# A kernel of attention and MLP on one Trainium2 core: another dealing of weight pieces, another order of MLP blocks, idle products, and an earlier order of v

## The chip, the cores and the metric

The kernel runs on 1 core of one Trainium2 chip. The metric is the device time of one execution in microseconds (us). A time is given as the median of the runs with the lowest and highest in brackets. All runs quoted here are of the fast state, but for one of `budget_mid_xt_first`, which is named there.

Before: 677.28 us (677.25 to 677.75, 3 runs).

## The reference, cut to what matters

```python
# attention, q k v f_logit: (4 batches, 8 heads, 768 tokens, 48)
f = 1 / (1 + exp(-f_logit))
for t in range(S):
    state = f[:, :, t, :, None] * state + einsum('bhd,bhe->bhde', k[:, :, t], v[:, :, t])
    y[:, :, t] = einsum('bhd,bhde->bhe', q[:, :, t], state)
x = y.transpose(0, 2, 1, 3).reshape(3072, 384)
# MLP, w_in: 384 x 2048, w_out: 2048 x 384 (scaled by numpy to float64)
h = x @ w_in
out = (h * sigmoid(1.702 * h)) @ w_out
```

## The kernel before

The sequence is cut into 12 attention units of 256 tokens. Each unit loads f, q and k (`raw`) and v (`vn`, and one `vl` per level), makes scores level by level, then the states (`st`), then the result `y`. ScalarE copies y out of PSUM into `yT`, and six DMA orders bring it into `xT`, the MLP's input. The MLP products (`h = xT @ w_in`, `o = g @ w_out`) of earlier units are put between the attention parts as filling, counted in columns. A whole MLP of a unit is `UNIT` = 24576 columns, some 41 us of TensorE by the 0.43 us that 256 columns took.

The weights arrive as float64 bits and are turned to float32 on VectorE: 32 pieces, in pairs of ten steps. Pieces are converted beside the first four attention units, and MLP blocks (a quarter of a unit's MLP each) can only be run when their pieces are done.

```python
def load_raw(n, j, engine=nc.sync):          # f, q or k of unit n: four orders on one queue
    ...
def load_vn(n): ...                          # v of unit n: from the third unit on, one order
def to_x(y, x, ng):                          # yT to xT: six orders on the same queue
    for h in range(2):
        most, rest = y(h)
        nc.sync.dma_start(out=x[h * D:(h + 1) * D]..., in_=most)          # L591
        ... nc.sync.dma_start(out=x[D2 + p:D2 + p + w, c]..., in_=...)    # L596, twice

def mlp_h(n, ffs, g):
    ...
    return [(U, lambda ff=ff, c=c: one(ff, c), ...) for ff in ffs for c in range(NK)]

# in the attention unit n (cut): the order in which its loads are sent
#   "states":     if n + 1 >= N_TURN: load_vn(n + 1)
#   begin_k:      if n: load_raw(n + 1, 2)       # k, run at the end of unit n - 1
#   "inter":      y += state products; yT copies; to_x(...)

def merge(n, fill, columns, share, pieces=0, hold=0, by=1.0):
    ...   # the parts of unit n, with `columns` of filling and `pieces` conversions between them
    converting = {"W": 3, "T": 3, "B": 1} if n < N_FILL - 1 else {"W": 3, "V": 4, "S": 3, "T": 1, "B": 1}
    ...

merge(0, fill, 0, steady, 8)
fill += mlp_blocks((0, 0)) + mlp_blocks((0, 1))
merge(1, fill, UNIT // 2 - LAG // 2, steady, 10, hold=1)
fill += mlp_blocks((1, 0), (1, 1)) + mlp_blocks((0, 2), (1, 2))
merge(2, fill, UNIT, steady, 8)
fill += mlp_blocks((2, 0), (2, 1)) + mlp_blocks((2, 2), (0, 3)) + mlp_blocks((1, 3), (2, 3))
merge(3, fill, 3 * UNIT // 2 - LAG // 2, steady, 6, by=0.7)
```

The units are called first to twelfth below; the first is n = 0. "States end" is the end of the last L542 of a unit. Other lines that come up: L383 the scores (`sc`), L562 the products of y with the states, L570 the copies of y into `yT`, L619 the products h, L645 the products o, L625 on VectorE the gate (`g`, from h and its sigmoid), L218 to L227 the weight conversions. In a kernel with an edit ahead of a line its number is up to seven higher (L626 for L619, say).

Of the kernel before, what the change touches and what calls it, by code (L numbers as in the profile page):

```python
# [9 lines left out]
F32 = mybir.dt.float32  # L10
# [13 lines left out]
def kernel(  # L24
# [32 lines left out]
    nc = tc.nc  # L57
    B, H, S, D = q.shape
    DM = H * D
    DFF = moe_w_in.shape[1]  # L60
    P = 128
    C = 64
    G = 128
    U = 256
# [6 lines left out]
    NL = len(LEV)  # L71
    NK = DM // P
    NFF = DFF // P
    FG = 4
    PAIRS_AHEAD = 3
    N_FILL = 3
# [10 lines left out]
    ps = ctx.enter_context(tc.tile_pool(name="ps", bufs=1, space=bass.MemoryType.PSUM))  # L87
# [16 lines left out]
    ident = const.tile([P, P], F32, name="ident")  # L104
# [3 lines left out]
    masks = const.tile([P, NL, 64], F32, name="masks")  # L108
# [40 lines left out]
    for r in range(NGR):  # L149
        ffs = range(r * FG, (r + 1) * FG)  # L150
        for ff in ffs[::2]:
            f = slice(ff * P, (ff + 2) * P)
# [8 lines left out]
    NPC = 2 * FG  # L161
# [68 lines left out]
    def convert():  # L230

        if state["begin"] < len(pairs) and len(todo) <= NOP:
            begin_pair(state["begin"])
            state["begin"] += 1
        if todo and todo[0]:
            todo.pop(0)()
        if todo and todo[0] is None:
            todo.pop(0)
            state["done"] += 2
            fetch_weights()  # L240
# [34 lines left out]
    def load_vl(n, l):  # L275

        if n >= NALL:
            return
        t = vls[n, l] = ld.tile([P, DM], F32, tag=f"vl{l}", name=f"vl_{n}_{l}")
        if n < N_TURN:  # L280
            pt = ps.tile([P, DM], F32, tag="mm", name=f"tv_{n}_{l}", bufs=4)
            for g in range(NG):
                nc.tensor.matmul(  # L283
                    pt[g * 64:(g + 1) * 64], lhsT=perm[:, l - 1, :] if l else ident[:, ::2], rhs=vns[n][:, g, :],
                    start=True, stop=True,
                )
            nc.scalar.copy(t, pt)
            return
        nc.sync.dma_start(out=t, in_=v_toks[n % 2].rearrange("(n two m) e -> two n m e", two=2, m=LEV[l])[0])
# [20 lines left out]
    serial = count()  # L310
# [295 lines left out]
    def width(n):  # L606

        return U + (n == NALL - 1)

    def mlp_h(n, ffs, g):  # L610
        t = {}

        def one(ff, c):
            if c == 0:
                if ff % FG == 0:
                    g[ff // FG] = mlp.tile([P, FG, width(n)], F32, tag="g", name=f"g_{n}_{ff}", bufs=6)
                t["ph"] = ps.tile([P, width(n)], F32, tag="mm", name=f"h_{n}_{ff}", bufs=4)
            ph = t["ph"]
            nc.tensor.matmul(  # L619
                ph, lhsT=w_in[:, c, ff * P:(ff + 1) * P], rhs=xTs[n][:, c, :], start=(c == 0), stop=(c == NK - 1)  # L620
            )
            if c == NK - 1:
                sg = mlp.tile([P, width(n)], F32, tag="sg", name=f"sg_{n}_{ff}")
                nc.scalar.activation(sg, ph, AF.Sigmoid, scale=1.702)  # L624
                nc.vector.tensor_tensor(g[ff // FG][:, ff % FG, :], ph, sg, ALU.mult)  # L625
                if width(n) > U:  # L626

                    by = g[ff // FG][:, ff % FG, U:]
                    if ff == 0:
                        g["last"] = mlp.tile([P, 1, DM], F32, tag="sum", name="sum_last", bufs=3)  # L630
                        nc.vector.tensor_scalar(g["last"][:, 0], w_out[:, 0, :], by, None, op0=ALU.mult)
                    else:
                        nc.vector.scalar_tensor_tensor(
                            g["last"][:, 0], w_out[:, ff, :], by, g["last"][:, 0], op0=ALU.mult, op1=ALU.add
                        )
        return [(U, lambda ff=ff, c=c: one(ff, c), ff // FG * NPC + ff % FG + 1) for ff in ffs for c in range(NK)]

    def mlp_o(n, ffs, g, done):

# [39 lines left out]
    def mlp_block(n, r):  # L679

        g, ffs = {}, range(r * FG, (r + 1) * FG)

        def done(tt, po):
            if r == 0 and tt == 0:
                sums[n] = mlp.tile([P, U // P, DM], F32, tag="sum", name=f"sum_{n}", bufs=3)
            acc = sums[n][:, tt]
            if r == 0:
                nc.scalar.copy(acc, po)
            else:
                nc.vector.tensor_tensor(acc, acc, po, ALU.add)  # L690
            if r == NGR - 1:
                store(n, tt, acc)
        return mlp_h(n, ffs, g), mlp_o(n, ffs, g, done)

    def mlp_blocks(*blocks):

        hs, os = zip(*(mlp_block(n, r) for n, r in blocks))
        return sum(hs, []) + sum(os, [])


    units = [attention(n) for n in range(NALL)]
    LAG = 18 * DM

    def parts_of(n):

        parts = list(units[n][1])
        _, inter = parts.pop()
        if n:
            kind, scores = parts[0]
            _, ahead = units[n - 1][1][-1]  # L710
            parts[0] = kind, lambda: (ahead(), scores())
        if n < N_TURN:

            def with_v(l):
                kind, fn = parts[l]
                return kind, lambda: (fn(), load_vl(n, l) if n == 0 or l else None)
            parts[:NL] = [with_v(l) for l in range(NL)]
        if n + 1 < NALL:
            begin_f, begin, begin_k, begin_gates = units[n + 1][0]
            i = len(parts)  # L720
            if n + 1 < N_FILL:

                parts.append(("K", lambda: (begin_k(), begin_gates(), load_vl(n + 1, 0) if n + 1 < N_TURN else None)))
                parts.insert(i - 4, ("B", begin))
                parts.insert(i - 5, ("B", begin_f))
            else:
                kind, states = parts.pop()
                parts += [("B", begin_k), (kind, lambda: (states(), begin_gates()))]
                parts.insert(i - 3, ("B", lambda: (begin_f(), begin())))
        else:  # L730
            parts.append(("W", inter))
        return parts

    def merge(n, fill, columns, share, pieces=0, hold=0, by=1.0):



        parts = parts_of(n)
        total = sum(share(kind) for kind, _ in parts)
        converting = {"W": 3, "T": 3, "B": 1} if n < N_FILL - 1 else {"W": 3, "V": 4, "S": 3, "T": 1, "B": 1}  # L740
        total_ops = sum(converting.get(kind, 0) for kind, _ in parts)
        held = sum(share(kind) for kind, _ in parts[:hold])
        at = at_ops = done = ops = 0
        for kind, fn in parts:
            ready = state["done"]
            fn()
            at += share(kind)
            at_ops += converting.get(kind, 0)
            n_ops = min(int(pieces * NOP * at_ops / (by * total_ops)), pieces * NOP) - ops
            ops += n_ops  # L750
            first, n_columns = done, max(0, columns * (at - held) / (total - held) - done)

            def some(end):
                nonlocal done
                while fill and done < end and fill[0][2] <= ready:
                    w, emit, _ = fill.pop(0)
                    emit()
                    done += w
            for i in range(n_ops):
                some(first + n_columns * i / n_ops)  # L760
                convert()
            some(first + n_columns)
# [4 lines left out]
    UNIT = NFF * NK * U + U // P * NFF * DM  # L767
# [12 lines left out]
        load_raw(1, j)  # L780
    load_vn(1)
    fill = []
    merge(0, fill, 0, steady, 8)
    fill += mlp_blocks((0, 0)) + mlp_blocks((0, 1))
    merge(1, fill, UNIT // 2 - LAG // 2, steady, 10, hold=1)
    fill += mlp_blocks((1, 0), (1, 1)) + mlp_blocks((0, 2), (1, 2))
    merge(2, fill, UNIT, steady, 8)
    fill += mlp_blocks((2, 0), (2, 1)) + mlp_blocks((2, 2), (0, 3)) + mlp_blocks((1, 3), (2, 3))
    merge(3, fill, 3 * UNIT // 2 - LAG // 2, steady, 6, by=0.7)
    fill_order.close()  # L790
    for n in range(3, NALL):
        fill += mlp_unit(n)
# [33 lines left out]
```

## Time and profile before

| | before |
|---|---|
| time | 677.28 us (677.25 to 677.75) |
| span of the profile | 674.0 us |
| TensorE busy | 652.6 us |
| states end, first, second, third unit | 43.9, 84.8, 141.4 us |
| TensorE at half clock, 11 to 160 us | 13.7 us |

The last row is from the table by stretch in steps of half a microsecond. The share of the chain of work that ended last, by engine:

```profile
PE 89%; DVE 7%; ACT 2%; issue 1%; DMA 1%; SPq 0%; DVEq 0%; ACTq 0%
```

DMA has 1% of it. The DMA queue's own view, in order of time, round the end of the second unit (start, length of the order on the queue, line, what is moved, how many):

```profile
72.52 0.69 SPq L289 DMA_DIRECT2D vl<-v_tok  x1
74.29 5.47 SPq L179 DMA_DIRECT2D bits<-in_moe_w_out_dram  x2
79.85 0.57 SPq L289 DMA_DIRECT2D vl<-v_tok  x1
80.47 0.46 SPq L303 DMA_DIRECT2D vn<-v_tok  x1
83.12 2.58 SPq L257 DMA_DIRECT2D raw<-in_k_dram  x4
87.07 0.59 SPq L591 DMA_DIRECT2D xT<-yT  x1
87.70 1.22 SPq L596 DMA_DIRECT2D xT<-yT  x2
89.12 0.51 SPq L591 DMA_DIRECT2D xT<-yT  x1
90.57 1.38 SPq L596 DMA_DIRECT2D xT<-yT  x2
```

I did not read this view before predicting; it is shown here because the case turned on it. The reader is to see the order: v of the third unit, the four orders of k of the fourth unit, then the six of xT. The yT copies began at 85.28, and the last xT landed at 93.88 by the chain: 8.6 us later. A length here is only the time of the order on the queue, not that to the landing: below, an order of 0.46 us lands after 13.66.

### The profile page before, as it was taken

To read this page: it belongs to the slowest core of one execution; us is meant where nothing else is said; L and a number is where in the kernel's file an instruction comes from. 1 tells how busy PE (TensorE), PEld (TensorE's weight loads), DVE (VectorE), ACT (ScalarE), POOL (GpSimd) and SP (SyncE) were. 2 spreads that over 40 slices of the span, in tenths; PEclk is the share of its full clock that TensorE was granted. 3 is DMA by queue.
4 is the path that set the end of the run, shared out by engine and by line. 5 is a ranking of instruction groups with operands and counts; after the bars stand their busy time and mean duration, and the time that the engine had idled before them with its cause. 6 is when DMAs were issued, how large, how long until landed. Compare 5 with 4: busy or idle time off the path is not lost.

```text
span 674.0 us, 19354 instructions
## 1 busy us (share of the span) xinstructions
PE 652.6 (97%) x8514; PEld 486.5 (72%) x8514; DVE 378.4 (56%) x675; ACT 226.4 (34%) x459; POOL 50.3 (7%) x116
## 2 busy tenths in 40 slices
PE   5879999999999999999999999999999999999997
PEld 4656766757777886886886886876886786786774
DVE  3999877887666546545546546445446444430440
ACT  4564443343134233333333233233233233231210
POOL 3020020010002002002002002002002001000000
PEclk9789999999999999999999999999999999999999
DMA  8877973571063535415415415415414103001000
GB/s 193 226 192 193 240 160 89 152 185 37 24 159 107 154 66 149 109 38 148 115 33 152 110 37 148 113 37 144 115 37 115 37 24 84 15 1 36 13 1 24
DMA packets 67551, 67.62 MB, mean 100 GB/s; under 512 B 30410, under 2 KB 61290, under 8 KB 67466
## 3 DMA queue, kind: packets, MB, share of 16 engines
q1 hardware_dynamic: 67466, 66.38, 38.6%
q8 instruction: 67, 1.10, 0.7%
q14 instruction: 18, 0.15, 0.1%
HBM read 56.92 MB, written 8.65 MB: 97 GB/s over the span
## 4 chain that ended last, share of the span: by engine, by line
PE 89%; DVE 7%; ACT 2%; issue 1%; DMA 1%; SPq 0%; DVEq 0%; ACTq 0%
PE h L619 37%; PE o L645 35%; PE sc L383 5%; PE y L447 5%; PE t L338 2%; PE y L562 2%; PE tkn L504 1%; PE sc L522 1%; DVE s L218 1%; DVE A L409 1%; DMA xT<-yT 1%; PE tv L283 1%; ACT yT L570 1%; DVE X L436 1%; DVE X L438 1%
## 5 line engine op out<-in xcount | busy, mean ns | idle before, releaser
L619 PE MATMUL h<-xT,w_in 128*128 128x256 f32 (+1 forms) x1152 | 261.1, 382 | 1.1 <-DVE sum L690 0.8
L645 PE MATMUL o<-w_out,g 128*128 128x384 f32 x768 | 259.6, 491 | 0.9 <-DVE g L625 0.9
L619 PEld LDWEIGHTS h<-xT,w_in 128*128 128x128 f32 x1152 | 215.8, 190 | 36.8 <-issue 3.5
L645 PEld LDWEIGHTS o<-w_out,g 128*128 128x128 f32 x768 | 143.0, 190 | 94.5 <-issue 2.2
L625 DVE TENSOR_TENSOR g<-h,sg 128x256 f32<-128x256 f32 (+1 forms) x192 | 80.8, 422 | 133.1 <-ACT sg L624 132.6
L624 ACT ACTIVATE sg<-h 128x256 f32<-128x256 f32 (+1 forms) x192 | 73.2, 383 | 169.4 <-PE h L619 164.1
L422 ACT COPY Kc<-X 128x512 f32<-128x512 f32 x69 | 45.9, 666 | 123.7 <-DVE X L438 87.3
L438 DVE TENSOR_TENSOR X<-X,tot 128x1024 f32<-128x1024 f32 x45 | 55.2, 1226 | 54.8 <-PE sc L383 50.1
L409 DVE TENSOR_TENSOR A<-sc,masks 128x512 f32<-128x512 f32 x72 | 46.7, 679 | 0.0
L326 DVE STREAM_TRANSPOSE X<-raw 128x1024 f32<-128x1024 f32 x18 | 36.7, 2039 | 16.7 <-PE y L562 13.9
L447 PE MATMUL y<-A,vl 64*48 64x64 f32 x2304 | 41.7, 219 | 0.0
L447 PEld LDWEIGHTS y<-A,vl 64*48 64x48 f32 x2304 | 36.8, 122 | 5.3 <-issue 5.0
L375 POOL TENSOR_TENSOR tot<-F 128x512 f32<-128x512 f32 x12 | 12.5, 1039 | 340.5 <-DVE st L539 327.9
L383 PE MATMUL sc<-X,Kc 48*64 48x64 f32 x1344 | 29.0, 224 | 6.8 <-ACT Kc L422 4.6
L383 PEld LDWEIGHTS sc<-X,Kc 48*64 48x64 f32 x1344 | 24.6, 138 | 13.8 <-ACT Kc L422 7.2
L570 ACT COPY yT<-y 48x512 f32<-48x512 f32 x48 | 27.8, 580 | 20.0 <-PE y L562 19.4
L331 ACT ACTIVATE F<-F 128x1024 f32<-128x1024 f32 x9 | 9.5, 1057 | 49.0 <-DVE F L326 49.0
L375 POOL TENSOR_TENSOR tot<-tot 128x256 f32<-128x256 f32 (+4 forms) x60 | 23.7, 395 | 4.7
L542 DVE TENSOR_TENSOR st<-st,sc 128x192 f32<-128x192 f32 x44 | 15.6, 354 | 15.1 <-PE sc L522 13.7
L338 PE MATMUL t<-ident,raw 128*64 128x128 f32 x288 | 19.6, 298 | 4.4 <-DMA raw<-in_f_logit_dram 4.4
L338 PEld LDWEIGHTS t<-ident,raw 128*64 128x64 f32 x288 | 18.4, 153 | 7.0 <-issue 6.1
L664 ACT COPY osb<-o 128x384 f32<-128x384 f32 x18 | 8.6, 478 | 41.5 <-PE o L645 41.5
(66 smaller groups left out, 385.0 us busy)
## 6 DMA issues: line engine op xcount, KB each, us to landing
vl<-v_tok SPq DMA_DIRECT2D x60, 192.0 KB, 2.8
bits<-in_moe_w_out_dram SPq DMA_DIRECT2D x8, 768.0 KB, 9.8
bits<-in_moe_w_in_dram SPq DMA_DIRECT2D x8, 576.0 KB, 7.9
v_tok<-in_v_dram SPq DMA_DIRECT2D x10, 384.0 KB, 4.3
vn<-v_tok SPq DMA_DIRECT2D x10, 384.0 KB, 6.0
xT<-yT SPq DMA_DIRECT2D x24, 144.0 KB, 2.7
raw<-in_f_logit_dram SPq DMA_DIRECT2D x18, 192.0 KB, 3.9
raw<-in_q_dram SPq DMA_DIRECT2D x18, 192.0 KB, 3.1
```

Source lines behind the costliest of these rows:

```text
L326: nc.vector.transpose(out.rearrange("p (a i j) -> p a j i", a=NP, j=R), raw[:, j].rearrange("p a (j d) -> p (a j) d", j=R)[:, :, :32],)
L338: nc.tensor.matmul(pt[h * HS:(h + 1) * HS, jj, :], lhsT=by_pair[j][:, h, x:x + HS], rhs=ident, start=True, stop=True)
L375: nc.gpsimd.tensor_tensor(tn, t2[:, :, 0], t2[:, :, 1], ALU.mult)
L383: nc.tensor.matmul(out[g * HS:(g + 1) * HS, h, a, :], lhsT=lhs(h, a * U + g * G), rhs=rhs(h, a * U + g * G), start=True, stop=True,)
L409: nc.vector.tensor_tensor(A[:, :, c:c + w].rearrange("p h (x t) -> p h x t", t=64), t["sc"][:, :, c:c + w].rearrange("p h (x t) -> p h x t ...
L422: nc.scalar.copy(c.rearrange("p (n m) -> p n m", m=m), X[:, j, :NA].rearrange("p (n two m) -> p n two m", two=2, m=m)[:, :, hf, :],)
L438: nc.vector.tensor_tensor(qk, qk, by, ALU.mult)
L447: nc.tensor.matmul(dst(h, g, a), lhsT=vls[n, u][g * 64:(g + 1) * 64, (2 * a + h) * D:(2 * a + h + 1) * D], rhs=A(h, g, a), start=(start an ...
L619: nc.tensor.matmul(ph, lhsT=w_in[:, c, ff * P:(ff + 1) * P], rhs=xTs[n][:, c, :], start=(c == 0), stop=(c == NK - 1))
L624: nc.scalar.activation(sg, ph, AF.Sigmoid, scale=1.702)
L625: nc.vector.tensor_tensor(g[ff // FG][:, ff % FG, :], ph, sg, ALU.mult)
L645: nc.tensor.matmul(t["po"], lhsT=g[ff // FG][:, ff % FG, tt * P:(tt + 1) * P], rhs=w_out[:, ff, :], start=(ff == ffs[0]), stop=(ff == ffs[ ...
```

## The change

The intent is to spread the weight conversions more evenly over the first four units (6, 6, 12, 8 pieces for 8, 10, 8, 6), so that the first unit, in which VectorE is the bound (busy for all of the 17 us from 17 to 34), and the second get shorter. The filling of these units shrinks with it, and the MLP blocks come in the order in which their weights are ready. Small parts go along: orders of v earlier, five idle products that are to keep the array's clock up, and the three products of an h as one piece of filling.

```diff
-        return [(U, lambda ff=ff, c=c: one(ff, c), ...) for ff in ffs for c in range(NK)]
+        return [(NK * U, lambda ff=ff: [one(ff, c) for c in range(NK)], ...) for ff in ffs]
...
+    def keep_up(times):
+        pt = ps.tile([P, NL * 64], F32, tag="mm", name=f"idle_{next(serial)}", bufs=4)
+        for _ in range(times):
+            nc.tensor.matmul(pt, lhsT=ident, rhs=masks.rearrange("p l t -> p (l t)"), start=True, stop=True)
...
-                return kind, lambda: (fn(), load_vl(n, l) if n == 0 or l else None)
+                ls = (l,) if n == 0 else {0: (1, 2, 3), 1: (4,), 2: (5,)}.get(l, ())
+                return kind, lambda: (fn(), [load_vl(n, i) for i in ls], keep_up(2 - l // 2) if n == 0 and l < 3 else None)
...
-        converting = {"W": 3, "T": 3, "B": 1} if n < N_FILL - 1 else ...
+        converting = {"W": 3, "T": 2, "B": 1, "K": 2} if n < N_FILL - 1 else ...
...
-    merge(0, fill, 0, steady, 8)
-    fill += mlp_blocks((0, 0)) + mlp_blocks((0, 1))
-    merge(1, fill, UNIT // 2 - LAG // 2, steady, 10, hold=1)
-    fill += mlp_blocks((1, 0), (1, 1)) + mlp_blocks((0, 2), (1, 2))
-    merge(2, fill, UNIT, steady, 8)
+    merge(0, fill, 0, steady, 6)
+    fill += mlp_blocks((0, 0))
+    merge(1, fill, UNIT // 8, steady, 6, hold=1)
+    fill += mlp_blocks((1, 0)) + mlp_blocks((0, 1), (1, 1)) + mlp_blocks((0, 2), (1, 2))
+    merge(2, fill, UNIT * 7 // 8, steady, 12)
     fill += mlp_blocks((2, 0), (2, 1)) + mlp_blocks((2, 2), (0, 3)) + mlp_blocks((1, 3), (2, 3))
-    merge(3, fill, 3 * UNIT // 2 - LAG // 2, steady, 6, by=0.7)
+    merge(3, fill, 2 * UNIT - LAG // 2, steady, 8, by=0.5)
```

Below, "the plan" is the dealing, the budgets of columns, the order of blocks and the table `converting`.

More of the change, by code (lines that the diff above doesn't have):

```diff
@@ L635, in one @@
                         )
-        return [(U, lambda ff=ff, c=c: one(ff, c), ff // FG * NPC + ff % FG + 1) for ff in ffs for c in range(NK)]
+        return [(NK * U, lambda ff=ff: [one(ff, c) for c in range(NK)], ff // FG * NPC + ff % FG + 1) for ff in ffs]
     def mlp_o(n, ffs, g, done):
@@ L739, in merge @@
         total = sum(share(kind) for kind, _ in parts)
-        converting = {"W": 3, "T": 3, "B": 1} if n < N_FILL - 1 else {"W": 3, "V": 4, "S": 3, "T": 1, "B": 1}
+        converting = {"W": 3, "T": 2, "B": 1, "K": 2} if n < N_FILL - 1 else {"W": 3, "V": 4, "S": 3, "T": 1, "B": 1}
         total_ops = sum(converting.get(kind, 0) for kind, _ in parts)
```

## The prediction

> **What bounds the kernel now.** I read the page's busy shares first, then the table by stretch, then the order of time of VectorE and TensorE where the table shows a gap. The page:
>
> ```profile
> PE 652.6 (97%) x8514; PEld 486.5 (72%) x8514; DVE 378.4 (56%) x675; ACT 226.4 (34%) x459; POOL 50.3 (7%) x116
> ```
>
> TensorE is busy for 652.6 of 674.0 us, so only 21.4 us is idle. From 209 us on it never waits, apart from the last 3.5 us (the final store). Hence nothing after the first quarter can gain: no product of the real work is removed. The table by stretch (stretch, length, busy us of PE, PEld, DVE, ACT, POOL, then granted clock, DMA share, GB/s):
>
> ```profile
> 12.46:20.00 7.54, 4.35 (x104) 2.19 (x104) 7.06 (x15) 2.87 (x7) 2.06 (x5) 1.00 1.08 261
> 23.00:28.50 5.50, 5.00 (x85) 3.83 (x85) 5.50 (x14) 2.64 (x6) 0.00 (x0) 0.50 0.75 177
> 28.50:38.60 10.10, 9.33 (x292) 7.56 (x290) 10.10 (x24) 7.12 (x13) 0.38 (x2) 1.00 0.92 234
> 44.80:47.50 2.70, 0.03 (x3) 0.01 (x2) 2.55 (x5) 2.63 (x6) 2.39 (x5) 0.64 0.32 70
> 47.50:52.40 4.90, 4.90 (x72) 3.27 (x73) 4.53 (x11) 2.05 (x4) 0.10 (x1) 0.50 0.53 114
> 52.40:84.00 31.60, 31.60 (x532) 22.55 (x530) 27.73 (x65) 15.45 (x32) 0.38 (x2) 1.00 0.88 221
> ```
>
> Two things are to be seen. In the first attention unit (12.5 to 44 us) VectorE is busy without a break: it bounds there, TensorE only looks busy. And twice TensorE runs at half clock, 21.7 to 28.5 and 45.6 to 52.4 us. What VectorE does in the first unit, in order of time (start, length):
>
> ```profile
> 29.69 0.68 DVE L435 TENSOR_TENSOR X<-X,tot 128x512 f32<-128x512 f32 x1
> 30.35 0.69 DVE L436 TENSOR_TENSOR X<-X,tot 128x512 f32<-128x512 f32 x1
> 30.95 0.68 DVE L409 TENSOR_TENSOR A<-sc,masks 128x512 f32<-128x512 f32 x1
> 31.55 0.62 DVE L225 TENSOR_SCALAR a<-s 128x384 int32<-128x384 int32 x2
> 32.09 1.02 DVE L226 SCALAR_TENSOR_TENSOR a<-bits,a 128x384 f32<-128x384 uint32 x2
> 33.03 1.02 DVE L227 TENSOR_TENSOR w_out<-a,s 128x384 f32<-128x384 f32 x2
> ```
>
> A level costs 1.8 us of its own work (L435, L436, L409 follow at 0.60), and then the weight conversions (L218 to L227). From starts: a pair of L222 or L225 takes 0.54, a pair of L218, L226 or L227 0.94. Ten such steps, one pair of pieces, take 3.90 us. And TensorE around its gaps:
>
> ```profile
> 20.64 0.69 PE L383 MATMUL sc<-X,Kc 48*64 48x64 f32 x32 [1.96 <-ACT Kc L422]
> 47.49 1.13 PE L383 MATMUL sc<-X,Kc 48*64 48x64 f32 x32 [2.67 <-ACT Kc L422]
> 151.72 4.69 PE L619 MATMUL h<-xT,w_in 128*128 128x256 f32 x20 [0.78 <-DVE sum L690]
> ```
>
> [...]
>
> **The change part by part.** I walked the new order of VectorE and TensorE with the durations above.
>
> *First unit, 6 pieces for 8.* Ahead of the states (L537) VectorE now has 31 conversion steps for 44. The 13 removed are one pair (3.90) plus one L222 (0.27) and two L218 (0.94): 5.1 us, all on the path. The first levels stay as they were, because the copy Kc waits behind two activations for a weight DMA that lands at 18.98. By the walk the states end at 39.1 for 43.9.
>
> *Idle products.* Five of 128x384. A product of that shape takes 0.645 us (32 records, 16 products, in 10.32 us), 3.2 us together. Two fall into the gap of 1.64 us at 15.1, two into that of 1.96, one into 0.5. They hide behind VectorE and should keep the clock up; but 3.15 us of cold time saved there is gain only where TensorE bounds, so I count none.
>
> *Orders of v early.* Three products of v (0.8 us each) move into the 2.67 us gap where ScalarE copies yT (4 x 0.58) and Kc. The gap shrinks to some 0.4, and the second cold stretch (4.9 us busy at half clock, so 2.45) should go.
>
> *Second unit.* Steps 50 to 30, and the fill falls from 8832 columns to 3072; 256 columns of a product take 0.43 us, and so TensorE has 24 us of work for 34. VectorE has 30 x 0.39 = 11.7, 18 x 0.6 = 10.9, gates 1.4 and 0.6 lost to GpSimd's turn: 24.6 us. It now bounds, and waits some 2.5 us for the first gate: the first h needs xT, which landed 6.5 us after the yT copies began. States end 39.1 + 27.2 + 3.1 (eight L539/L542) = 69.4 (before: 84.8, with 10.4 us more MLP done).
>
> *Third unit.* Steps 35 to 55. VectorE: 55 x 0.39 = 21.5, 18 x 0.6 = 10.8, twelve gates 4.1, sums 1.0, three transposes 5.8, a promotion 1.15 and 0.6: 45 us, against 40 for TensorE. It bounds again; with 2.8 us of waits the states end at 69.4 + 47.8 + 3.1 = 120.3. Before it was 141.3, having done 8 h (1.3 each) and 8 o (0.65) more: 15.6 us. Like for like 125.7 becomes 120.3: **5.4 us gained**, nearly all from the first unit.
>
> *Fourth unit.* Here I expect a new wait. After the first scores come eight h in a row, and the four PSUM buffers "mm" let only four (5.2 us) run before the first gate has freed one. That gate stands on VectorE behind ten conversion and sum steps (4.3), two promotions with the ScalarE copies between (3.8), two evacuations (1.2) and GpSimd's turn (some 1.3): 10.8 us after the states. TensorE is there after 6.5: a wait of 4.3 us, where before 16 o came first and 0.78 was lost. **Cost 3.5 us**, and the clock may fall in it (3 chances in 4, some 2.5 us: 1.9). *Products of an h together* only shifts points of interleaving by under 0.9 us; I count zero.
>
> Sum: -5.4 + 3.5 + 1.9 = 0.0, so by the bare walk 677.3.
>
> **The rivals.** (1) *TensorE takes the whole saving*: the conversions hide in the third and fourth units, and most idle time between 12 and 152 us (some 13.5 us) plus the cold 5.6 goes. For it: VectorE is only 56% busy over the span. Against: those units would be at 45 of 48 us. It would give 660 to 664. (2) *VectorE becomes the bound of unit three*, with transposes and sums behind conversions holding PSUM buffers: idle time only moves. For it the sums above. 675 to 680. (3) *Weight DMA paces it*: the DMA share is near 1 up to 45 us, and conversions wait. Against: pieces are needed later than before, and only 2.5 us of waiting for bits is in the trace. No change, 677.
>
> **Range and chances.** The walk charges each wait in full and lets nothing slip by, and eighths of a unit look like numbers tuned by measurement; so between the walk (677.3) and half of rival 1's gain I choose a gain of 3.3 us: 674.0. One wait of 4 us more or less on each side and an uncertain clock give 667 to 679. For 2% the gain would have to be 13.5 us, nearly all there is: 0.04. A loss of 13.5 us would need several new waits like that of the fourth unit: 0.01.
>
> **What would show it.** Right: the first states end near 39 us; the clock is full to 45 us; the gap ahead of the second unit's second scores is under 1 us; VectorE is 90% busy or more from 70 to 118 us; and an h in the fourth unit waits 3 to 5 us for a gate L625, perhaps with half clock after it. From then on no waits. Wrong: if that wait is under 1 us the time is near 669; if TensorE is idle under 2 us in the third unit, VectorE's steps overlap better than I walked; if cold stretches stay in the first two units, idle products do not do what they are for, and the time is above 677.

## The result, and the profile after

The changed kernel took **687.02 us** (683.47 to 688.08, 4 runs) beside 677.51 us (677.25 to 679.1, 4 runs) of the kernel before. The ratio is 1.0126, 95% interval 1.0084 to 1.0168. A ratio is the mean time of one kernel's fast runs over the mean of the other's of the same rounds, so it is not quite the ratio of the medians. In a later job the same kernel took 684.5 us (`after_again` below). It is slower by about 1%, within the 2% of "same", and outside the predicted range.

The page of the changed kernel, busy shares and then the chain that ended last:

```profile
PE 659.2 (96%) x8524; PEld 491.5 (72%) x8524; DVE 381.5 (56%) x675; ACT 227.1 (33%) x459; POOL 51.3 (7%) x116
...
PE 82%; DVE 7%; DMA 6%; SPq 2%; ACT 1%; issue 1%; DVEq 0%; ACTq 0%
```

The span grew by 12.1 us in this execution: TensorE is busy 6.6 us longer (4.7 of it the idle products) and idle 5.5 us longer. DMA with its queue has gone from 1% of the chain to 8%. What TensorE waited for:

```profile
PE h L619 <- DMA xT<-yT: 5.1, 2, 2.6
...
PE y L562 <- issue: 3.4, 2, 1.7
PE y L562 <- DVE st L542: 3.0, 2, 2.5
PE h L619 <- DVE g L625: 1.7, 1, 1.7
```

Two waits for xT, 5.1 us together, are new: before, that row had 0.3. The DMA queue in order of time, at the same place as before:

```profile
70.34 0.82 SPq L179 DMA_DIRECT2D bits<-in_moe_w_in_dram  x2
71.26 0.56 SPq L289 DMA_DIRECT2D vl<-v_tok  x1
71.88 0.46 SPq L303 DMA_DIRECT2D vn<-v_tok  x1
73.04 3.51 SPq L257 DMA_DIRECT2D raw<-in_k_dram  x4
79.08 0.59 SPq L591 DMA_DIRECT2D xT<-yT  x1
80.29 4.63 SPq L596 DMA_DIRECT2D xT<-yT  x2
85.60 0.52 SPq L591 DMA_DIRECT2D xT<-yT  x1
86.16 1.83 SPq L596 DMA_DIRECT2D xT<-yT  x2
```

The yT copies began at 77.04, so the first order should go near 79 and the last near 82. Instead the queue stands still between 80 and 85.6. The chain says on what:

```profile
71.88 13.66 DMA vn<-v_tok
...
85.60 2.94 DMA xT<-yT
...
88.68 5.81 PE h L619 x18
```

The load of v took 13.66 us to land, and the fourth order of xT is sent at the moment it has landed. Why the one should wait for the other is told by counting orders. The queue's waits of this trace name, for the xT orders, weights (2.5 us), a vl (3.5) and vn (0.6). Going back eight orders from the first xT one comes to a weight load, from the third to the vl of 71.26, from the fourth to vn. By this count an order of xT that stood still went out when the order eight before it had landed. The packed trace, which also holds what `prof` does not print, says why: the program has eight semaphores for the landing of its orders and deals them out in turn, so that in both kernels each of the 347 later orders (of 355) signals the same one as the order eight before it, and the xT orders that stood still waited for just that one. In both traces all 347 went out after the last landing signal of the order eight before; in the changed kernel the third of xT at 84.42 us, the vl having landed at 84.40, and the fourth at 85.60, vn having landed at 85.54. That comes from this program's eight semaphores; no run here shows a limit of the chip. In the kernel before the same count holds: there two xT orders waited, for 1.2 us together, for loads of k, which are eight back from the fifth and sixth.

The changed kernel stretches its loads over less time. From the vl order ahead of q's four to the end of k's orders it takes 14.2 us (62.37 to 76.55), and before the same run of orders, with one weight order more, took 19.9 us (65.78 to 85.70). The stretch of 18 us round it, before and then after, by the table by stretch (length, busy us of PE, PEld, DVE, ACT, POOL, clock, DMA share, GB/s):

```profile
72.00:90.00 18.00, 17.11 (x305) 12.62 (x294) 15.67 (x37) 10.49 (x21) 3.63 (x6) 1.00 0.94 223
```

```profile
72.00:90.00 18.00, 12.92 (x201) 8.88 (x196) 12.35 (x26) 7.04 (x12) 3.19 (x6) 0.89 0.80 156
```

TensorE lost 4 us in these 18, and VectorE 3. The clock fell too, from 1.00 to 0.89.

Where the span went, from the ends of the states. The walk is the one of the prediction; its last part is that of before with the 15.6 us of moved MLP work, 3.5 for the fourth unit's wait and 1.9 for the clock added, so that its sum is, as in the prediction, the span of before:

| | before | the walk | after |
|---|---|---|---|
| first unit's states end | 43.9 | 39.1 | 40.4 |
| second unit | 40.9 | 30.3 | 34.5 |
| third unit | 56.6 | 50.9 | 59.4 |
| from there to the end | 532.6 | 553.6 | 551.8 |
| span | 674.0 | 673.9 | 686.1 |

### The profile page after: what moved, and what is told of

It is laid out like the page before. It is cut to its first block, busy times and chain, and to the rows that moved or that the text cites. A ratio compares the mean times of both kernels' runs of the same rounds, so it can differ in the third digit from the quotient of the medians.

```text
span 686.1 us, 19380 instructions
## 1 busy us (share of the span) xinstructions
PE 659.2 (96%) x8524; PEld 491.5 (72%) x8524; DVE 381.5 (56%) x675; ACT 227.1 (33%) x459; POOL 51.3 (7%) x116
## 4 chain that ended last, share of the span: by engine, by line
PE 82%; DVE 7%; DMA 6%; SPq 2%; ACT 1%; issue 1%; DVEq 0%; ACTq 0%
PE h L619 35%; PE o L645 34%; PE sc L383 4%; PE y L447 4%; DMA vn<-v_tok 2%; PE y L562 2%; PE sc L522 1%; DMA bits<-in_moe_w_out_dram 1%; PE tkn L504 1%; DMA bits<-in_moe_w_in_dram 1%; DMA xT<-yT 1%; DVE s L218 1%; DVE a L226 1%; SPq L179 1%; SPq L250 1%
## 5 line engine op out<-in xcount | busy, mean ns | idle before, releaser
L619 PEld LDWEIGHTS h<-xT,w_in 128*128 128x128 f32 x1152 | 218.9, 192 | 44.0 <-issue 6.4
L625 DVE TENSOR_TENSOR g<-h,sg 128x256 f32<-128x256 f32 (+1 forms) x192 | 81.1, 424 | 152.4 <-ACT sg L624 151.7
L505 ACT COPY kn<-tkn 128x512 f32<-128x512 f32 x24 | 13.8, 583 | 36.0 <-PE tkn L504 35.9
L356 POOL COPY q_last<-X 128x4 f32<-128x4 f32 x12 | 10.3, 859 | 188.1 <-DVE X L326 139.1
L542 DVE TENSOR_TENSOR st<-st,sc 128x192 f32<-128x192 f32 x44 | 15.6, 354 | 14.7 <-PE sc L522 13.2
## 6 DMA issues: line engine op xcount, KB each, us to landing
vn<-v_tok SPq DMA_DIRECT2D x10, 384.0 KB, 13.7
```

Source lines behind the costliest of these rows:

```text
L619: nc.tensor.matmul(ph, lhsT=w_in[:, c, ff * P:(ff + 1) * P], rhs=xTs[n][:, c, :], start=(c == 0), stop=(c == NK - 1))
L625: nc.vector.tensor_tensor(g[ff // FG][:, ff % FG, :], ph, sg, ALU.mult)
```

## The experiments

After the first comparison fifteen more runs were made, in four jobs: fourteen other kernels, and the changed one again. Every one gave a correct result. "Delay" below is the time from the start of the second unit's yT copies to the landing of the xT that the chain names, the last that h waited for: 8.6 us before (85.28 to 93.88), 11.5 in the changed kernel (77.04 to 88.54).

My theory at the start was that the plan does it, by the xT transfers standing behind loads and by the fall of the clock; the rivals were the small parts (idle products, early v, h in one piece).

### plan_alone and plan_undone: which part

The kernel before with the plan alone, and the changed kernel with the old plan alone put back:

```diff
 # plan_alone: before.py, with
-    merge(1, fill, UNIT // 2 - LAG // 2, steady, 10, hold=1)
+    merge(1, fill, UNIT // 8, steady, 6, hold=1)
 # ... and the rest of the plan; plan_undone: after.py with the reverse of it
```

> The kernel before with only the plan changed: pieces 6, 6, 12, 8 with the new conversion table, the block order and the column budgets. Theory P (the plan causes the loss: it takes some 10 us of MLP work out of the second unit, so the same loads and conversions meet in less time, and the orders that carry xT wait behind bulk loads): slower than before by 8 to 12 us, 685 to 689, with two waits of h for xT of about 2.5 us and a third cold stretch. Rival S (the small parts, above all idle products and products of an h together, cause it): 675 to 679, no wait for xT over 1 us.

Measured: 688.58 us (685.41 to 690.27), ratio 1.015 (1.0112 to 1.0189). The time is as theory P has it; of the two waits for xT that it named, the trace has one (2.5 us), and it has four cold stretches (half clock) for three.

> The changed kernel with the old plan put back; orders of v early, idle products and products of an h together stay. Theory P: the loss is gone, 674 to 679. Rival S: 684 to 688.

Measured: 676.96 us (675.27 to 679.63), ratio 0.9976 (0.9939 to 1.0013). In the profile, which fell on the slowest of the four runs (679.63 us), the third unit took 61.3 us, with a wait of 3.6 us for xT and a delay of 10.3: late xT is not wholly the plan's own. But the plan alone has the whole loss in time, and the small parts together change nothing that these runs can tell. The rival that blamed the small parts has fallen.

### no_idle: the changed kernel without the idle products

```diff
-[load_vl(n, i) for i in ls], keep_up(2 - l // 2) if n == 0 and l < 3 else None)
+[load_vl(n, i) for i in ls])
```

> The changed kernel without the five idle products (4.7 us of TensorE time as traced, partly cold). Theory P: within 2 us of the changed kernel, 685 to 689, since VectorE bounds the first unit. Rival S: 681 to 683, the 4.7 us come back.

Measured: 689.96 us (686.75 to 690.66), ratio 1.0167 (1.0131 to 1.0203). This is just above theory P's 685 to 689 and far from the rival's 681 to 683. The changed kernel had 1.0126 in another job and the intervals meet, so this settles no more than that the idle products are not the loss. The time at half clock is 20.5 us with them and without.

### xt_first: the loads of k and v moved behind xT

The k of the third and fourth unit and the v of the third are kept back in a list and ordered after the six orders of xT. The data and every dependence stay.

```diff
-            if n:
+            if n in (1, 2):
+                deferred.append(lambda: load_raw(n + 1, 2))
+            elif n:
                 load_raw(n + 1, 2)
...
-            if n + 1 >= N_TURN:
+            if n == 1:
+                deferred.insert(0, lambda: load_vn(n + 1))
+            elif n + 1 >= N_TURN:
                 load_vn(n + 1)
...
             to_x(lambda h: (yT[rows(h), :NK], lambda r, d: yT[r:r + d, NK]), xT[:, :, :U], NG)
+            while deferred:
+                deferred.pop(0)()
```

> The changed kernel with the k loads of units 2 and 3 and the vn load of unit 2 ordered after the xT orders in place of before them. Theory P: the two waits of h for xT (2.5 and 2.6 us) and VectorE's idle behind them (4.0 and 4.4 us before a gate) shrink to under 1.5 us each; 680 to 684. Rival S: no change, 685 to 689.

Measured: 680.08 us (679.56 to 681.25), ratio 1.0033 (1.0005 to 1.0061). The delay fell from 11.5 to 8.5 us and the third unit from 59.4 to 52.9 us. That is 7 us less than the first measurement of the changed kernel and 4.4 less than the later one (`after_again`), by nothing but the order of loads. The time is what P expected, and so is the second wait for xT (0.66 us); the first did not shrink below 1.5 us (2.26 for 2.50).

### pieces_old: the old dealing with the new budgets

```diff
-    merge(1, fill, UNIT // 8, steady, 6, hold=1)
+    merge(1, fill, UNIT // 8, steady, 10, hold=1)
 # also 8, 8, 6 pieces for 6, 12, 8 in the other units, by=0.7, and the old table `converting`
```

> The changed kernel with the weight pieces dealt 8, 10, 8, 6 and the conversion steps placed as before; the new budgets of MLP columns and the new order of blocks stay. Theory T (transfers: the second unit is so short that the xT transfers of its end stand behind bulk loads): the second unit gets longer again (50 conversion steps for 30, some 8 us more of VectorE), so the loads are spread over more time and the waits of h for xT shrink to under 2.5 us together (from 5.1). But with 10 pieces and few columns TensorE idles in the second unit. T makes it 679 to 685. Rival B (it is the small budget of columns in the second unit, not the dealing, that loses time: TensorE has too little to do): 685 or more, with more idle time of TensorE in the second unit. Rival D (the dealing alone is at fault): near 677, like the kernel before.

Measured: 690.9 us (689.96 to 691.63), ratio 1.0185 (1.0153 to 1.0218): rival B's number, and a miss for mine. The second unit is as long as before (40.2 us) and has hardly any filling, so the time that the new dealing frees was not there to pay for the smaller budget. The waits for xT fell to 3.4 us, more than expected of T; other waits took their place (y for st 3.8, sc for A 3.5, tkn for X 3.3). So dealing and budgets belong together; this run does not show the dealing to be at fault.

### budget_mid: more filling in the second unit

```diff
-    merge(1, fill, UNIT // 8, steady, 6, hold=1)
+    merge(1, fill, UNIT // 4, steady, 6, hold=1)
-    merge(2, fill, UNIT * 7 // 8, steady, 12)
+    merge(2, fill, UNIT * 3 // 4, steady, 12)
```

> The changed kernel with a quarter of a unit of MLP columns in the second attention unit for an eighth, and three quarters for seven eighths in the third; pieces as changed. Theory T (xT behind bulk loads) expects the waits of h for xT to stay at 4 to 5.5 us, as the same loads are issued in the same order and VectorE still has 30 conversion steps: 685 to 688, less than 2 us from the changed kernel. Rival B (TensorE starved by the small budget): 3072 more columns, 5 us of work, fill idle time in the second unit, 681 to 684.

Measured: 695.15 us (690.6 to 696.5), ratio 1.0241 (1.0197 to 1.0285). Neither theory had this. TensorE in order of time shows why (in brackets the wait and what ended it):

```profile
90.00 5.66 PE L619 MATMUL h<-xT,w_in 128*128 128x256 f32 x18 [13.29 <-DMA xT<-yT]
```

The h that needs xT starts at 90.00; the delay was 13.6 us. In the changed kernel 16 products o lay beside this delay; here the larger budget had used them up in the second unit, and nothing was left to run. So the wait that TensorE shows is not the size of the trouble. The delay is, and the wait is what the filling leaves of it. That was the error in my expectation of 4 to 5.5 us.

### budget_mid_xt_first: the same with the loads moved

> The kernel with a quarter of a unit of columns in the second unit (695.15 us; one h waited 13.3 us for xT in it, 78 to 90 us), now with the loads of k for the third and fourth unit and of v for the third ordered after the xT transfers. Theory T (xT of the second unit lands at 89 to 90 us in both new plans because its orders stand behind bulk loads; the order of the MLP only decides how much work lies beside that): the 13.3 us shrink to 5 to 7 us, the time from yT copies to landed xT when nothing stands ahead, and the time falls by at least 7 us, to 683 to 688. Rival (the wait is the budget's own, for products that need an xT of the same unit at once): it stays over 10 us and the time over 690.

Measured: 688.48 us (684.04 to 694.33), but the run of 694.33 is listed as slow; the median of the three fast runs is 687.21. The ratio, of fast runs alone, is 1.0135 (1.0103 to 1.0167). In the trace:

```profile
80.54 6.68 PE L626 MATMUL h<-xT,w_in 128*128 128x256 f32 x18 [6.01 <-DMA xT<-yT]
```

The wait went from 13.29 to 6.01 us and the delay from 13.6 to 6.4, near the 6.5 that the prediction had taken for the first unit's xT. The third unit fell from 64.5 to 58.2. The fast median is within T's 683 to 688, near its upper edge.

### plan_undone_no_idle: early v and h in one piece alone

> The changed kernel with the old plan and without the five idle products: what is left of the change is the early order of v and the products of an h together. With the idle products the cold time was 6.8 us for 13.7 in the kernel before. If the idle products keep the clock up, the cold time goes back to 10 us or more and the time rises by 1 to 3 us over 676.96. If the early order of v does it, cold time stays near 7 us and the time at 676 to 677.5.

Measured: 678.51 us (677.25 to 679.77), ratio 1.0001 (0.9968 to 1.0034). The time at half clock went down, to 3.4 us from 6.8, so in this pair the idle products do not keep the clock up. The time is 1.5 us more, with overlapping intervals. What the idle products are worth stays open: they may give 1 to 3 us in both plans, by what means these runs do not show.

### plan_undone_xt_first, plan_undone_xt_second and before_xt_second: the old plan with the loads moved

The first moves the loads of both units, as `xt_first` does; the other two only those of the second unit (`n == 2` for `n in (1, 2)` in the diff of `xt_first`).

> The changed kernel with the old dealing, budgets and order of blocks, and with the loads of k for the third and fourth unit and of v for the third ordered after the xT transfers. The kernel with the old plan alone took 676.96 us, 3.9 us of it in two waits of h for xT. Theory T: these waits shrink to under 1.5 us and the time to 673.5 to 675.5, below both kernels. Rival (in the longer second unit the bulk loads do not delay xT, it lands late for the weights' transfers instead): waits of 3 to 4 us stay and the time is 676 to 678.

Measured: 675.86 us (675.48 to 681.49), ratio 0.9988 (0.9941 to 1.0034). The later wait is gone, but the first xT is now waited for, 2.65 us. No order of that xT waited for an earlier one here, so the trace does not show what makes it late. The time lies between the two expectations.

> The changed kernel with the old plan, and with the loads moved behind xT in the second unit alone (v of the third unit and k of the fourth); in the first unit k stays ahead. With both moved the time was 675.86 us, with a new wait of 2.65 us for the first xT, whose orders then came next behind the large weight loads, and the later wait gone. Theory T: neither wait is there (under 1 us together for xT), and the time is 672.5 to 675, below both kernels. Rival[...]: 675 to 677.5.

Measured: **674.9 us** (673.5 to 675.87, 6 runs), ratio 0.9956 (0.994 to 0.9973). This is faster than both kernels, by 0.44% of the one before. The waits of its TensorE:

```profile
PE t L339 <- DMA raw<-in_f_logit_dram: 4.3, 1, 4.3
PE h L626 <- DMA xT<-yT: 1.6, 3, 0.8
PE sc L386 <- DVE A L412: 1.4, 3, 0.7
```

The expectation was under 1 us for xT and it is 1.6 in three small pieces; the time is at the top of the expected range.

> The kernel before with the same two loads moved behind xT in the second unit. It waits only 0.3 us for xT, so theory T gives it nothing: 676.5 to 678. Rival (a cheaper order of loads helps every version, so xt_first's gain says nothing about the plan): it gains 2 us or more, 675.5 or less.

Measured: 676.2 us (675.72 to 677.42, 6 runs), ratio 0.998 (0.9965 to 0.9994). The kernel before gains 0.2%, barely told from nothing; the time lies between the two expectations (676.5 to 678, and 675.5 or less). Its third unit is the same (56.3 for 56.6). Under the new plan the same move is worth 6 to 7 us of the third unit. The old plan with the small parts lies between: its third unit took 61.3 and 61.2 us in `plan_undone` and `plan_undone_no_idle`, with waits of 3.6 and 3.8 us for xT, and 55.6 in both profiles with the loads moved, but the medians of `plan_undone` and `plan_undone_xt_second` are only 2.1 us apart. Both profiles with the late xT fell on the slowest run of their kernel, so it may come in some executions and not in others; these profiles cannot say.

### vn_last, both_second, k_last and after_again: which load it is

These are the changed kernel with v alone, both, k alone, and nothing moved behind the xT of the second unit.

> The changed kernel (687.02 us) with one load alone moved behind the xT transfers: v of the third unit, the one that took 13.7 us and ended just as the third order of xT was sent; the loads of k stay ahead. Theory V (the xT orders wait for the oldest of the eight before them, and that was this load): xT lands 3 us or more earlier, the second wait of h for xT (2.6 us) goes below 1 and the time falls to 680 to 684. Rival K (any bulk load ahead of xT does it, the engines being full): k, ordered at 73 to 76.5 us, takes its place; the wait stays over 2 us and the time at 685 to 688.

Measured: 681.38 us (680.88 to 683.2), ratio 1.0057 (1.0038 to 1.0076). The time fits V, the trace does not: the second wait for xT is 4.1 us, the delay 11.1, the third unit 58.4. (In the changed kernel v ended as the fourth order of xT was sent, not the third as the expectation has it.) Its chain:

```profile
67.77 11.05 DMA vl<-v_tok
...
78.88 3.57 DMA xT<-yT
...
82.54 7.08 PE h L624 x18
```

With v gone, the order eight before the fourth xT is a vl, and this one takes 11 us. The waiting has only changed its name.

> The changed kernel with v of the third unit and k of the fourth both ordered after the xT of the second unit; the loads of the first unit as changed. Theory W (the xT orders stand behind any big load among the eight orders before them while the engines are full, so both have to go): the time from the first yT copy to the h that needs xT falls from 11.5 to 9 us or less, the third unit takes 52 to 54 us for 59.4, and the time is 679 to 682, as with all three loads moved (680.08). Rival V (v alone did it): no better than v alone, 681.4, with a delay near 11 us. Rival N (the first unit's order counts): 684 or more.

Measured: 679.88 us (676.99 to 684.23), ratio 1.0037 (0.9987 to 1.0086), delay 8.5, third unit 53.1, all as theory W has it.

> The changed kernel with k of the fourth unit alone moved behind xT of the second unit; v of the third stays ahead. Theory W: v still stands ahead, so the delay from yT copies to xT stays at 10.5 us or more and the third unit at 57 us or more; the time is 683 to 688. Rival K (the four k loads, ordered last before xT, fill the engines just when xT should move): delay of 9 us or less, third unit under 55 us, 679 to 682.

Measured: 679.73 us (677.57 to 687.35), ratio 1.0044 (0.9985 to 1.0103), delay 9.2 (78.98 to the landing at 88.19 by the chain), third unit 52.8. Rival K's numbers, but for a delay just over its 9, and theory W is wrong in saying that both loads have to go. The profile fell on the slowest of the four runs (687.35 us): its first and second unit took 43.4 and 35.6 us, though the edit changes nothing before the end of the second, so only the delay and the third unit are compared. The reason is again in the queue's order of time:

```profile
75.36 0.56 SPq L289 DMA_DIRECT2D vl<-v_tok  x1
75.98 0.69 SPq L303 DMA_DIRECT2D vn<-v_tok  x1
80.78 0.59 SPq L596 DMA_DIRECT2D xT<-yT  x1
81.42 2.09 SPq L601 DMA_DIRECT2D xT<-yT  x2
83.61 0.54 SPq L596 DMA_DIRECT2D xT<-yT  x1
84.19 1.22 SPq L601 DMA_DIRECT2D xT<-yT  x2
85.51 2.94 SPq L257 DMA_DIRECT2D raw<-in_k_dram  x4
```

Without the four orders of k, vn stands six before the last xT, and no xT order reaches it by going back eight. So vn need not be moved: it is the number of orders between that made it stand in the way. This count also fits `vn_last`. The load that k adds to the engines goes with it, and no run parts the two wholly. But the trace shows that v is late without it: it took 10.3 us to land here too (at 86.30), and by then the last of the six xT orders had gone out (84.83). Nor is it the transfer of xT that got much shorter: from its order to its landing the xT that h waited for took 2.9 to 4.2 us in six profiles of the plan with k ahead, and 2.6 to 4.0 in four with k behind. What came sooner is its order, 3.7 to 5.2 us after the yT copies began for 7.6 to 9.4.

> The changed kernel once more, unchanged, on this chip in these rounds. [...]its median is within 684 to 689 and its second unit (first to second end of the states) may take 31 to 37 us where the first profile has 34.5; the third unit, where the loads stand ahead of xT, takes 57.5 to 60 us and the delay from yT copies to xT is 10.5 to 13 us in any case. If it comes out at 682 or less, the gain of vn_last is nothing but such a difference.

Measured: 684.5 us (682.39 to 684.95), ratio 1.0088 (1.0068 to 1.0108), delay 12.9, third unit 60.3, second unit 30.8 for 34.5 in the first profile. Time and delay are within what was expected, the two units just outside. So the second unit differs by 3.7 us between two executions of one kernel, which is why the gain of `vn_last` may not be put down to its edit; the third unit and the delay do not differ so. With k ahead of xT the third unit took 58.0 to 60.3 us in five profiles of the plan (`plan_alone` 58.0, `no_idle` 59.1, and those of the table); with k behind, 52.8 to 53.1 in three (`xt_first` 52.9). In the time of the same job, `k_last` and `both_second` are 4.8 and 4.6 us below `after_again`, though the slowest run of `k_last` (687.35) is above all four of its runs.

| moved behind xT | delay | third unit | time |
|---|---|---|---|
| nothing (changed kernel) | 11.5 | 59.4 | 687.02 |
| nothing (`after_again`) | 12.9 | 60.3 | 684.5 |
| v (`vn_last`) | 11.1 | 58.4 | 681.38 |
| k (`k_last`) | 9.2 | 52.8 | 679.73 |
| v and k (`both_second`) | 8.5 | 53.1 | 679.88 |

## Why the prediction was wrong, point by point

**The step that failed** is in the paragraphs on the second and third unit. They took xT to land "6.5 us after the yT copies began" and charged 2.8 us of waits to the third unit, by which its states would end "69.4 + 47.8 + 3.1 = 120.3". The 6.5 is of the first unit's xT (44.39 to 50.95, when h started, without a wait); the second unit's took 8.6 us in the same trace, and was not looked at. In the new plan, with k ahead, it took 10.7 to 13.6 us, and with the new dealing the third unit 58.0 to 64.5 us for 50.9. The work was walked rightly: in the third unit of the changed kernel VectorE was busy for 48.6 us, and the walk has 45 and 3.1. The term that failed is the waits: of the unit's 59.4 us VectorE was idle for 10.8, not 2.8. With k behind xT alone it was idle for 4.4 of 52.8 us, so 6 to 7 us of the 8 come back by moving k.

**Rival 3** (weight DMA paces it) was turned down with "pieces are needed later than before, and only 2.5 us of waiting for bits is in the trace". The argument looked at what waits for weights. It should have looked at what waits behind all loads on the same queue: the attention's own loads of the second unit were pushed into 14.2 us for 19.9.

**Second unit** 34.5 us for 30.3: by 4.2 us too low in the first profile. But `after_again`, `plan_alone`, `vn_last` and `both_second` had 30.8, 31.3, 31.3 and 31.5, so there the walk was nearly right. The first profile, `xt_first`, `k_last` and `no_idle` had 34.5, 33.6, 35.6 and 36.8; each of these has a cold stretch in this unit (51.9 to 55.3 us in the first profile) and a wait of 2.3 to 2.9 us for the first xT (1.47 in `after_again`). Which of the two brings the other these runs do not show.

**First unit:** 40.4 and 40.0 us for 39.1 in the two profiles of the changed kernel, and 39.0 to 41.0 in the others of the plan but `k_last` (43.4). Right to about 2 us but for that one.

**Fourth unit:** the predicted wait of h for the gate L625 came, at 1.7 us for 4.3, and with 2.6 and 2.2 in `both_second` and `k_last`. The clock falls to half in all of them, as given 3 chances in 4 (from 121 to 128.5 us in `both_second` and from 130 to 137 in `k_last`), but earlier than I put it: from 133.5 to 141 us in the changed kernel, after a wait of 2.5 us of y for the states at 132, which I had not seen. From the third states to the end it was 551.8 us, 1.8 below the walk.

**The bare walk was better than the prediction.** Its sum was 677.3 us, "a gain of 3.3 us" was then taken off by choice, towards rival 1. `both_second`, in which the delayed xT is mended, has its states' ends at 39.0, 70.5 and 123.7 us (walk: 39.1, 69.4, 120.3) and 553.4 us from there to the end (walk: 553.6). Its median is 679.88 us. So even without the DMA trouble the plan would have won nothing: the first unit's gain is paid out again in the fourth, as the walk has it. That is rival 2's range of 675 to 680, and with its reason: from 70 to 118 us VectorE was busy for 44.4 of 48 us in `both_second`, over the 90% that I gave as a sign. In the changed kernel it was 38.4, since VectorE too stood idle behind the late xT. Rival 1 (TensorE takes the whole saving) is far off.

**Idle products** were to "keep the clock up"; that they would was my assumption. The first cold stretch came before them, from 14.3 to 17.8 us, and the first of them ran cold: 4.7 us of busy time together for the predicted 3.2. That was too low in any case, as they took 4.0 us at full clock in `both_second`. There were five cold stretches for two, 20.5 us for 13.7. The sign "if cold stretches stay in the first two units, idle products do not do what they are for, and the time is above 677" was right in both halves, but the second does not follow from the first: `no_idle` is no faster. The longest gap of TensorE just ahead of a cold stretch was 1.96 us in the kernel before (the stretch from 21.68 us) and 2.50 in the changed one (from 51.89 us). The cold time differs from one execution to another: two profiles of the changed kernel have 20.5 and 17.1 us at half clock, at partly different places.

**Signs:** the gap ahead of the second unit's second scores was to be under 1 us, and is 0.6, as the early orders of v were to do (2.67 before). Of the signs for a wrong prediction none was a wait for xT.

**Sums:** two sums are off by little (18 x 0.6 is 10.8, not 10.9; the parts ahead of the fourth unit's gate make 10.6, not 10.8), and no conclusion hangs on them. That each engine takes its operations in the order of the program was an assumption of the walk.

What stays open: the two breaks of 1.7 us in y L562 that the trace calls "issue" (3.4 us in the changed kernel; 2.1 to 2.8 in four versions of the plan with moved loads and none in `budget_mid_xt_first`; 0.26 at that place before). They come in most profiles of the new plan (but 0.6 us in `plan_alone` and 0.7 in `budget_mid`), but no experiment touched them. In the changed kernel they fell into stretches with DMA shares of 0.85 (36 to 44 us) and 1.05 (68 to 76). One thing the packed traces show: all 26 breaks of TensorE over 0.4 us that are called "issue", in 17 traces, begin within 1.1 us, before or after, of the end of a 16 KB transfer of the queue q8, "instruction"; in the changed kernel these ended at 41.05, 73.83 and 82.81 us, the breaks began at 40.82, 73.74 and 83.86, and the transfers around are 4 to 11 us apart. No run tests whether the one has to do with the other. Open too is what the idle products are worth, and whether anything but what the walk counts is in the remaining 2 us between `k_last` and the kernel before: the interval of that ratio holds 1.

## What to carry to other kernels

When a stage is made shorter, list not only its compute but every transfer that is ordered in it, in the order of the queue. A small transfer that something waits for should not stand behind large ones: in the new plan the delay of xT was 10.7 to 13.6 us with the loads of k ahead of it and 6.4 to 9.2 with them behind. How many orders lie between them counts too, where a program deals out a few semaphores in turn (eight here): with four orders fewer between v and xT (`k_last`) nothing of xT waited for v, though v took 10.3 us to land. A wait of the bounding engine shows only what the filling has left of a delay (13.29 us of 13.6 in `budget_mid`, 2.6 of 11.5 in the changed kernel); measure the delay itself, from the first copy to the landing, before deciding how much filling the stage needs.
